# A fused attention, mixture-of-experts and gated-MLP kernel: another order of the first loads and of the first weight splits

## The chip, the cores and the metric

The kernel runs on one core of a Trainium2 chip. The time is the device time of one execution in microseconds; three executions were timed, and one more was recorded by the profiler. The engines are PE (TensorE, with PEld for its weight loads), DVE (VectorE), ACT (ScalarE), POOL (GpSimd) and SP (SyncE, which here only issues transfers).

## The reference

Causal attention with a bias from running sums of s, then four experts of which every token takes a share, then a gated MLP:

```python
scores = scale * np.matmul(q, k.transpose(0, 1, 3, 2))        # batch 2, 8 heads, 576 rows, 64 wide
cum = np.cumsum(np.maximum(s, 0.0), axis=-1)
bias = -(cum[:, :, :, None] - cum[:, :, None, :])
scores = np.where(causal, -1e9, scores + np.minimum(bias, 0.0))
attn = softmax(scores); x = (attn @ v) as [1152, 512]
for e in range(4):
    h = np.maximum(x @ w1[e], 0.0)                             # w1 512 x 1024
    out += p[:, e:e + 1] * (h @ w2[e])                         # p: domain_probs, each row divided by its sum
result = (out @ w_a) * (out @ w_b) @ w_out                     # 512 x 1536, 512 x 1536, 1536 x 512
```

## The kernel before

Nearly all products are made of three matmuls on float32r operands: each factor is split into a high part (ACT copies it to the narrow type) and a low part (DVE or POOL subtracts the high part from the original). For a weight piece of 512 KB, loaded into a tile `raw`, these are `wh` (ACT, line 225) and `wl` (line 227, two subtractions of 128x512, by turns on POOL and on DVE). The program runs in four parts.

**The head** (lines 722 to 908) computes the attention of the first 256 rows of batch 0 for all eight heads: `head_scores` (sc, lines 770 and 773), `head_softmax` (lines 784 and 788), `head_turn` (transposes into `tr`, line 796, and a copy, 799 or 801), `head_av` (809), and for every second head `pair_out` (821 to 834), which divides, transposes (`xT`, 829, in a PSUM tile of the pool of `tr`) and leaves the rows of x in plain form (`x32`) and split (`xh`, `xl`). Beside it `sums_of_s` (line 838 on) makes the running sums of s for the other rows: four short operations on DVE (845 to 857), four on POOL, and three writes to a scratch tensor `ckD` in DRAM (867). The head's own sums are made first (746 to 755, with the high and low part in `cb`). Small matmuls on a constant tile (`lull`, line 712) keep PE occupied in between.

**Beside** (from about 26 us): expert 0 on those 256 rows with plain fp32 weights (`plain_expert`, line 1010, weights `w32` loaded at line 556), then expert 1, and interleaved with both the attention of all other rows. That attention is 24 jobs (three groups of rows by eight heads), each of two or three query tiles. For a job `load_job` fetches `qr`, `kr` (one buffer each, lines 565 and 566) and the bias rows of `kb` (from `ckD`, 567); `prep_job` makes `qh`, `qb`, `ks` (572 to 579) and writes the high part of k into `kb` by a transfer from SBUF to SBUF (`kb<-ks`, line 578); `load_v` fetches `vr`. A tile's scores are two matmuls for each part: line 605 with `ks`, and line 606 with `kb`, which adds the low part and the bias. Then follow a softmax (DVE line 616, ACT 628, 633, DVE 634, POOL 635), transposes (646), their split (661, 662) and the product with v (678).

**After**: expert 1 on the last rows, then experts 0, 2 and 3, then the gated MLP.

The order on each engine is set by a list scheduler from the order in which the code records the operations and from their estimated times. `in_order` (and `queued`, while `early[0]` is set) keeps operations in the order in which they were recorded among themselves. `issue_after` holds what is recorded under it until a named operation has been issued; in the kernel before, a block at the end holds the weight loads of `w2`, the first three raw pieces and `prep_job` of the first job until the last `pair_out`, and `attn_step` does so for the first three steps of the attention. PE, DVE, ACT, POOL and the queue on SP each run their list strictly from front to back.

The block of code that the change turns round, as it stands before:

```python
    early[0] = True
    load_job(jobs[0])
    load_v(jobs[0])
    load_job(jobs[1])
    with tc.issue_after(last["act"].ins), tc.issue_after(last["dve"].ins):
        queued(nc.sync.dma_start(out=pr, in_=dp))
        for m in range(2):
            load_w32("w2", m)
        for _ in range(3):
            load_next()
        prep_job(jobs[0])
        early[0] = False
        shares()
```

## Time and profile before

| | before |
|---|---|
| median of 3 runs | 756.69 us (755.91 to 764.51) |
| the profiled execution | 756.76 us, of it 755.0 us from the first to the last instruction |
| busy: PE, DVE, ACT, POOL | 715.8, 515.2, 324.6, 401.4 us |
| mean granted clock of PE | 0.982 of full speed |

The profiled execution's time is the span between its first and last instruction and 1.76 us around it. It lies 0.07 us above the median. PE is busy for 95% of the span. In the page's strip of 40 slices its share is 9 tenths nearly everywhere but for three slices early on, of which the lowest holds 2 tenths; there the granted clock is 5 and 9 tenths. Busy shares are means over very different stages, so the tables below go by stage.

### The profile page before, as it was taken

To read this page: it belongs to the slowest core of one execution; us is meant where nothing else is said; L and a number is where in the kernel's file an instruction comes from. 1 tells how busy PE (TensorE), PEld (TensorE's weight loads), DVE (VectorE), ACT (ScalarE), POOL (GpSimd) and SP (SyncE) were. 2 spreads that over 40 slices of the span, in tenths; PEclk is the share of its full clock that TensorE was granted. 3 is DMA by queue.
4 is the path that set the end of the run, shared out by engine and by line. 5 is a ranking of instruction groups with operands and counts; after the bars stand their busy time and mean duration, and the time that the engine had idled before them with its cause. 6 is when DMAs were issued, how large, how long until landed. Compare 5 with 4: busy or idle time off the path is not lost.

```text
span 755.0 us, 10970 instructions
## 1 busy us (share of the span) xinstructions
PE 715.8 (95%) x3880; PEld 623.7 (83%) x3880; DVE 515.2 (68%) x1056; ACT 324.6 (43%) x722; POOL 401.4 (53%) x332
## 2 busy tenths in 40 slices
PE   9628899999999999999999999999899999999998
PEld 5527679899989988888888888887788888898886
DVE  5317678876768677766565646679874788887764
ACT  4327778987743433222321323243545324242410
POOL 4336665765524553333312345598467779798600
PEclk9959999999999999999999999999999999999999
DMA  6284423344221131111101112123103132223003
GB/s 225 70 283 135 122 76 102 98 139 112 66 67 44 50 101 52 62 56 56 48 9 56 57 56 84 56 85 94 47 28 95 61 97 73 93 63 104 5 0 126
DMA packets 33580, 61.42 MB, mean 81 GB/s; under 512 B 3269, under 2 KB 17253, under 8 KB 33525
## 3 DMA queue, kind: packets, MB, share of 16 engines
q1 hardware_dynamic: 33045, 59.61, 25.4%
q10 hardware_dynamic: 480, 1.11, 0.4%
q8 instruction: 31, 0.51, 0.3%
q14 instruction: 24, 0.20, 0.1%
HBM read 55.11 MB, written 2.58 MB: 76 GB/s over the span
## 4 chain that ended last, share of the span: by engine, by line
PE 61%; DVE 14%; POOL 8%; issue 5%; ACT 3%; DMA 1%; POOLq 0%; ACTq 0%; DVEq 0%; SPq 0%
PE ps L269 29%; PE psq L269 19%; PE pst L269 4%; POOL wl L81 3%; PE av L678 3%; PE tr L646 2%; PE ps L1010 1%; POOL tp L162 1%; DVE tp L174 1%; DVE tp L170 1%; DVE h2l L81 1%; PE sc L605 1%; PE sc L606 1%; DVE acc L1185 1%; DVE tp L166 1%
## 5 line engine op out<-in xcount | busy, mean ns | idle before, releaser
L269 PE MATMUL ps<-wh,h2h 128*128 128x512 f32 x332 | 130.6, 393 | 0.0
L269 PE MATMUL ps<-wl,h2h 128*128 128x512 f32 x332 | 129.6, 390 | 0.0
L81 POOL TENSOR_TENSOR wl<-raw,wh 128x1024 fp32r<-128x1024 f32 x24 | 58.1, 2431 | 129.3 <-ACT wh L80 98.9
L269 PE MATMUL ps<-wh,h2l 128*128 128x512 f32 x332 | 125.8, 392 | 0.8 <-DVE h2l L81 0.8
L322 DVE SCALAR_TENSOR_TENSOR acc<-ps,pr,acc 128x512 f32<-128x512 f32 x111 | 82.2, 745 | 41.4 <-PE ps L269 40.7
L269 PE MATMUL psq<-xh,wh 128*128 128x448 f32 (+1 forms) x224 | 81.5, 364 | 0.0
L269 PE MATMUL psq<-xl,wh 128*128 128x448 f32 (+1 forms) x224 | 81.3, 363 | 0.0
L269 PE MATMUL psq<-xh,wl 128*128 128x448 f32 (+1 forms) x224 | 81.2, 363 | 0.0
L269 PEld LDWEIGHTS ps<-wh,h2l 128*128 128x128 f32 x332 | 62.2, 188 | 14.7 <-DVE h2l L81 1.6
L269 PEld LDWEIGHTS ps<-wh,h2h 128*128 128x128 f32 x332 | 62.4, 188 | 11.8 <-ACT h2h L80 0.3
L269 PEld LDWEIGHTS ps<-wl,h2h 128*128 128x128 f32 x332 | 62.4, 188 | 11.1
L333 ACT ACTIVATE h2h<-psq 128x448 fp32r<-128x448 f32 (+1 forms) x56 | 29.5, 531 | 96.0 <-PE psq L269 77.2
L81 POOL TENSOR_TENSOR wl<-sums,wh 128x1024 fp32r<-128x1024 f32 x24 | 58.2, 2423 | 4.9 <-ACT wh L80 4.8
L635 POOL TENSOR_SCALAR e<-e,r 128x448 f32<-128x448 f32 (+4 forms) x64 | 37.6, 591 | 36.0 <-DVE r L634 25.9
L80 ACT ACTIVATE wh<-raw 128x1024 fp32r<-128x1024 f32 x24 | 25.5, 1062 | 70.3 <-PE ps L269 53.5
L269 PE MATMUL psq<-tqh,wh 128*128 128x448 f32 x144 | 53.0, 368 | 1.8 <-DVE u L420 1.2
L269 PE MATMUL psq<-tql,wh 128*128 128x448 f32 x144 | 52.6, 365 | 0.0
L269 PE MATMUL psq<-tqh,wl 128*128 128x448 f32 x144 | 52.5, 364 | 0.0
L662 DVE TENSOR_TENSOR el<-tr,eh 128x512 fp32r<-128x512 f32 (+5 forms) x80 | 38.5, 484 | 18.2 <-ACT eh L661 17.4
L162 POOL TENSOR_SCALAR tp<-tp 128x512 f32<-128x512 f32 x24 | 47.3, 1986 | 5.6 <-ACT tp L161 5.6
L269 PE MATMUL pst<-xh,wh 128*128 128x256 f32 x160 | 44.9, 280 | 2.7 <-DVE xl L81 2.7
L420 DVE TENSOR_TENSOR u<-psq,s 128x448 f32<-128x448 f32 x48 | 29.6, 618 | 23.9 <-PE psq L269 22.3
(198 smaller groups left out, 1898.4 us busy)
## 6 DMA issues: line engine op xcount, KB each, us to landing
raw<-in_w SPq DMA_DIRECT2D x32, 512.0 KB
raw<-in_wa SPq DMA_DIRECT2D x12, 512.0 KB
raw<-in_wb SPq DMA_DIRECT2D x12, 512.0 KB
raw<-in_wo SPq DMA_DIRECT2D x12, 512.0 KB
kr<-in_kT SPq DMA_DIRECT2D x16, 288.0 KB
w<-in_w SPq DMA_DIRECT2D x8, 512.0 KB
vr<-in_v SPq DMA_DIRECT2D x16, 160.0 KB
kb<-ks SPq DMA_DIRECT2D x16, 144.0 KB
```

The source lines that it names most:

```text
L80: nc.scalar.activation(out=hi, in_=src, func=AF.Copy)
L81: lo_eng.tensor_tensor(out=lo, in0=src, in1=hi.bitcast(F32), op=ALU.subtract)
L162: nc.gpsimd.tensor_scalar(out=t.bitcast(F32), in0=t.bitcast(F32), scalar1=2.0**-15, scalar2=GMAX, op0=ALU.max, op1=ALU.min,)
L166: nc.vector.tensor_scalar(out=t, in0=t, scalar1=5, scalar2=2, op0=ALU.logical_shift_left, op1=ALU.logical_shift_right,)
L269: ins = nc.tensor.matmul(ps, lhsT=l, rhs=r, start=first and k == 0, stop=last and k == 2, skip_group_check=more)
L322: nc.vector.scalar_tensor_tensor(out=dst, in0=ps, scalar=share, in1=dst, op0=ALU.mult, op1=ALU.add)
L333: nc.scalar.activation(out=hh, in_=src, func=AF.Relu)
L420: nc.vector.tensor_tensor(out=out, in0=a, in1=b, op=ALU.add)
L635: nc.gpsimd.tensor_scalar(out=t.e, in0=t.e, scalar1=r, scalar2=1.0, op0=ALU.mult, op1=ALU.mult)
L646: ins = nc.tensor.transpose(ps[:, c - c0, :], t.e[:, k0 : k0 + P], ident)
L662: nc.vector.tensor_tensor(out=j.el[:, c0:c1, x], in0=src, in1=hi.bitcast(F32), op=ALU.subtract)
L678: ins = nc.tensor.matmul(ps[:, o:], lhsT=j.vs[:, c, :], rhs=e[:, c, o:], start=(m == 0), stop=(m == len(mms) - 1),)
```

## The change

- **First loads.** The head's second load of s moves from the last to the first place on ACT's queue. All eight loads of `w32` (w1 and w2 of expert 0) are issued on SP at the start; before, the four of w2 came behind the head. The load of the shares (`pr`) and the first three raw pieces follow right behind the first job's loads, held no longer by the head's end. The second job's loads come after them, and after `prep_job` of the first job with its `kb<-ks`.
- **Held splits.** The splits of the first two raw pieces (`gated` in `split_next`) and the first three steps of the attention are held until the last `pair_out` has been issued. Transfers stay in the recorded order until the third step of the attention.
- **Sums of s.** `sums_of_s` is recorded after the first head's scores and before its softmax, before after the second head. One of the two short subtractions for `cb` goes from DVE to POOL.
- **Own bank.** `xT` takes a tile of the pool of `av` (one buffer), not of `tr`.

The diff, without repeated context:

```diff
+    gate = []
+    nsplits = [0]
+    def gated(on):
+        x = ExitStack()
+        for i in gate if on else ():
+            x.enter_context(tc.issue_after(i))
+        return x
...
     def split_next():
         r, p_ = loaded.pop(0)
-        split_piece(r, *p_)
+        nsplits[0] += 1
+        with gated(nsplits[0] < 3):
+            split_piece(r, *p_)
...
     in_order(nc.sync.dma_start(out=sc[:, :NT0], in_=s[:, :NT0]))
+    in_order(nc.scalar.dma_start(out=sc[:NR, NT0:], in_=s[:NR, NT0:]))
...
     in_order(nc.scalar.dma_start(out=v65, in_=v0))
-    in_order(nc.scalar.dma_start(out=sc[:NR, NT0:], in_=s[:NR, NT0:]))
-    for m in range(2):
-        load_w32("w1", m)
+    early[0] = True
+    for key in ("w1", "w2"):
+        for m in range(2):
+            load_w32(key, m)
+    early[0] = False
...
-    for lo_ in (slice(32, NB), slice(96, NS)):
-        nc.vector.tensor_tensor(
+    for lo_, eng in ((slice(32, NB), nc.vector), (slice(96, NS), nc.gpsimd)):
+        in_order(eng.tensor_tensor(
...
-        ps = ps_t.tile([P, NT0], F32, tag="tr", name="xT")
+        ps = ps_a.tile([P, NT0], F32, tag="av", name="xT")
...
         if h < H:
             head_scores(h)
+        if h == 0:
+            sums_of_s()
+        if h < H:
             head_softmax(h)
...
-        if h == 1:
-            sums_of_s()
...
-        if n > 2:
-            attn_work(n)
-            return
-        with tc.issue_after(last["act"].ins), tc.issue_after(last["dve"].ins):
+        early[0] = early[0] and n < 3
+        with gated(n < 3):
             attn_work(n)
...
     load_job(jobs[0])
     load_v(jobs[0])
-    load_job(jobs[1])
+    queued(nc.sync.dma_start(out=pr, in_=dp))
+    for _ in range(3):
+        load_next()
     with tc.issue_after(last["act"].ins), tc.issue_after(last["dve"].ins):
-        queued(nc.sync.dma_start(out=pr, in_=dp))
-        for m in range(2):
-            load_w32("w2", m)
-        for _ in range(3):
-            load_next()
         prep_job(jobs[0])
-        early[0] = False
+        load_job(jobs[1])
         shares()
+    gate.extend((last["act"].ins, last["dve"].ins))
```

Two places of the resulting order carry the prediction. The first is SP's queue behind the writes of `ckD`. The names are those of the text above with the batch, head and tile behind them: `kb_0_2` belongs to the first job, `kb_1_2` to the second. Before:

```order
L567 DMA kb_0_2_421<-ckD 3x576
L585 DMA vr_0_2_425<-in_v 128x320
L565 DMA qr_1_2_428<-in_qT 128x384
L566 DMA kr_1_2_429<-in_kT 128x576
L567 DMA kb_1_2_430<-ckD 3x576
L1198 DMA pr<-in_dp 128x36
L556 DMA w_118<-in_w 128x1024 x2
L556 DMA w_119<-in_w 128x1024 x2
L156 DMA raw<-in_w 128x1024 x3
L578 DMA kb_0_2_421<-ks_0_2_449 64x576
L578 DMA kb_1_2_430<-ks_1_2_468 64x576
L565 DMA qr_2_2_475<-in_qT 128x384
```

With the change, from the same load on:

```order
L578 DMA kb_0_2_425<-ckD 3x576
L596 DMA vr_0_2_429<-in_v 128x320
L1209 DMA pr<-in_dp 128x36
L156 DMA raw<-in_w 128x1024 x3
L589 DMA kb_0_2_425<-ks_0_2_442 64x576
L576 DMA qr_1_2_449<-in_qT 128x384
L577 DMA kr_1_2_450<-in_kT 128x576
L578 DMA kb_1_2_451<-ckD 3x576
L589 DMA kb_1_2_451<-ks_1_2_468 64x576
L576 DMA qr_2_2_475<-in_qT 128x384
L577 DMA kr_2_2_476<-in_kT 128x576
L578 DMA kb_2_2_477<-ckD 3x576
```

The four loads of w2 are gone from this stretch (they stand at the queue's start), and the first job's `kb<-ks` has moved ahead of the second job's three loads; the three raw pieces are still ahead of it.

The second place is DVE behind the head, where the softmax of the first job's tiles (`e_0_2_2`, `e_0_2_3`, `e_0_2_4`) and the split of the second raw piece (`wl<-raw`) meet. Before:

```order
L573 SCALAR_TENSOR_TENSOR qb_83<-qr_1_2_428,qh_1_2_427 64x384
L877 TENSOR_SCALAR den<-den 128x9
L878 RECIPROCAL den<-den 128x9
L227 TENSOR_TENSOR wl<-raw,wh 128x512 x2
L616 ISA e_0_2_2_503,mn<-sc_0_2_2_481,causal 128x320
L616 ISA mn 128x1
L616 ISA e_0_2_3_525,mn<-sc_0_2_3_500,causal 128x448
L616 ISA mn 128x1
L634 RECIPROCAL r<-l 128x1 x2
```

With the change:

```order
L584 SCALAR_TENSOR_TENSOR qb_84<-qr_0_2_423,qh_0_2_422 64x384
L1040 TENSOR_SCALAR h_510<-ps_497 128x256
L627 ISA e_0_2_2_503,mn<-sc_0_2_2_481,causal 128x320
L627 ISA mn 128x1
L227 TENSOR_TENSOR wl<-raw,wh 128x512 x2
L627 ISA e_0_2_3_525,mn<-sc_0_2_3_500,causal 128x448
L627 ISA mn 128x1
L584 SCALAR_TENSOR_TENSOR qb_83<-qr_1_2_449,qh_1_2_448 64x384
L645 RECIPROCAL r<-l 128x1
L627 ISA e_0_2_4_556,mn<-sc_0_2_4_515,causal 128x320
L627 ISA mn 128x1
```

The split stood ahead of the first softmax and now stands between the first and the second; the second job's `qb` has gone behind both.

## Rows read from the trace of the kernel before

**Rows 1.** PE's waits over the whole run (us in total, times, longest).
```profile
PE sc L606 <- DMA kr<-in_kT: 17.9, 1, 17.9
PE sc L605 <- DVE mn L616: 4.7, 3, 2.2
...
PE tr L796 <- DVE eT L799: 0.7, 1, 0.7
```

**Rows 2.** Windows by stage (stretch: its us, engines' busy us, clock, DMA).
```profile
31.00:52.00 21.00, 1.60 (x8) 0.86 (x6) 3.34 (x7) 4.85 (x8) 8.18 (x13) 0.58 0.84 254
52.00:92.00 40.00, 35.03 (x168) 28.81 (x169) 26.20 (x76) 27.30 (x78) 24.30 (x26) 0.88 0.47 139
92.00:232.00 140.00, 136.90 (x930) 123.00 (x929) 105.73 (x331) 105.61 (x334) 79.16 (x103) 1.00 0.33 94
```

**Rows 3.** Timeline from 31 to 41 us (start, us, engine, line, operation).
```profile
31.22 0.68 ACT L577 ACTIVATE ks<-kr 128x576 fp32r<-128x576 f32 x1
...
32.03 1.39 POOL L579 TENSOR_TENSOR ks<-kr,ks 64x576 fp32r<-64x576 f32 x1 [0.31 <-ACT ks L577]
...
32.16 0.33 SPq L565 DMA_DIRECT2D qr<-in_qT  x1
33.45 0.33 SPq L566 DMA_DIRECT2D kr<-in_kT  x1
...
34.56 1.85 SPq L556 DMA_DIRECT2D w<-in_w  x4
34.59 0.52 ACT L572 ACTIVATE qh<-qr 128x384 fp32r<-128x384 f32 x1 [2.06 <-DMA qr<-in_qT]
...
36.15 0.68 ACT L577 ACTIVATE ks<-kr 128x576 fp32r<-128x576 f32 x1 [1.03 <-DMA kr<-in_kT]
...
36.46 2.60 SPq L156 DMA_DIRECT2D raw<-in_w  x3
...
39.10 1.38 SPq L578 DMA_DIRECT2D kb<-ks  x2
```

**Rows 4.** Windows of the two stretches in which the transfers are dense.
```profile
35.00:51.00 16.00, 0.00 (x0) 0.00 (x0) 2.02 (x5) 2.91 (x4) 5.19 (x10) 0.50 0.96 293
1.00:14.00 13.00, 12.42 (x57) 6.84 (x57) 7.36 (x29) 4.86 (x10) 5.69 (x19) 1.00 0.83 300
```

**Rows 5.** Timeline from 47 to 66 us.
```profile
47.20 2.48 POOL L227 TENSOR_TENSOR wl<-raw,wh 128x512 fp32r<-128x512 f32 x2 [7.33 <-ACT wh L225]
...
49.92 1.29 DVE L227 TENSOR_TENSOR wl<-raw,wh 128x512 fp32r<-128x512 f32 x2 [10.83 <-ACT wh L225]
...
51.97 0.98 PE L606 MATMUL sc<-kb,qb 67*128 67x320 f32 x2 [17.87 <-DMA kr<-in_kT]
...
60.54 0.40 PE L605 MATMUL sc<-ks,qh 128*128 128x320 f32 x1
...
61.07 2.96 POOL L227 TENSOR_TENSOR wl<-raw,wh 128x512 fp32r<-128x512 f32 x2
...
61.54 3.04 DVE L227 TENSOR_TENSOR wl<-raw,wh 128x512 fp32r<-128x512 f32 x2
...
65.44 0.39 PE L605 MATMUL sc<-ks,qh 128*128 128x256 f32 x1 [1.50 <-DVE mn L616]
```

**Rows 6.** Windows of 4 us from 52 to 84 us.
```profile
52.00:56.00 4.00, 4.00 (x10) 3.33 (x11) 1.37 (x6) 2.12 (x8) 1.08 (x2) 0.50 0.64 215
56.00:60.00 4.00, 4.00 (x17) 3.46 (x17) 1.79 (x6) 2.00 (x4) 1.66 (x3) 0.71 0.16 45
...
80.00:84.00 4.00, 2.82 (x14) 2.64 (x15) 3.85 (x15) 2.06 (x6) 1.68 (x3) 0.77 0.43 140
```

**Rows 7.** Timeline of VectorE in the head, 8 to 12 us.
```profile
8.13 0.29 DVE L784 CUSTOM_DVE_ANT_0 e<-sc,causal 128x128 f32<-128x128 f32 x1 [1.91 <-PE sc L773]
...
9.96 0.32 DVE L845 TENSOR_SCALAR s_sb<-s_sb 32x320 f32<-32x320 f32 x1 [0.63 <-DMA s_sb<-in_s]
...
11.96 0.27 DVE L784 CUSTOM_DVE_ANT_0 e<-sc,causal 128x128 f32<-128x128 f32 x1
```

More of the change, by code (lines that the diff above doesn't have):

```diff
@@ L750, in fused_kernel @@
     )
-    nc.vector.tensor_scalar(
+    in_order(nc.vector.tensor_scalar(
         out=cb, in0=cum[:NS, :NT0], scalar1=1.0, scalar2=1.0, op0=ALU.mult, op1=ALU.mult
-    )
-    for lo_ in (slice(32, NB), slice(96, NS)):
-        nc.vector.tensor_tensor(
+    ))
+    for lo_, eng in ((slice(32, NB), nc.vector), (slice(96, NS), nc.gpsimd)):
+        in_order(eng.tensor_tensor(
             out=cb[lo_], in0=cum[lo_, :NT0], in1=cb[lo_].bitcast(F32), op=ALU.subtract
-        )
+        ))
     nc.gpsimd.memset(v65[:, :, :, D : D + 1], 1.0)
@@ L844, in sums_of_s @@
             )
-        nc.vector.tensor_scalar(
+        in_order(nc.vector.tensor_scalar(
             out=sc[:NR, NT0:], in0=sc[:NR, NT0:], scalar1=0.0, scalar2=None, op0=ALU.max
-        )
+        ))
         nc.vector.tensor_tensor_scan(
```

## The prediction

> **What bounds the kernel now.** I read PE's waits first, since PE is busy for 95% of the span: one wait stands out, 17.9 us before the first matmul of line 606, and the next longest is 4.7 us in three pieces [rows 1]. Then the windows by stage, to see where the hole lies. From 31 to 52 us PE works 1.60 of 21.00 us; from 52 to 92 us 35.03 of 40.00 us at a mean clock of 0.88; from 92 to 232 us 136.90 of 140.00 us at full clock [rows 2]. So the kernel is bound by PE, but for one hole and a ragged stretch behind it. What is taken out of the hole comes off the end as long as the other engines can follow.
>
> The trace names `kr<-in_kT` as what ended the wait. The matmul of line 606 reads no `kr`; it needs `kb`, `qb` and its bank. The timeline shows what it really waits for. `ks` of the first job is ready at 31.22 + 0.68 = 31.90 us, but SP issues `kb<-ks` only at 39.10 us, behind four loads of w2 (34.56) and three raw pieces (36.46), and PE goes on at 51.97 us [rows 3, 5]. From 35 to 51 us the DMA engines are busy for 0.96 of the time at 293 GB/s, that is 4.7 MB in 16 us [rows 4]; the seven weight transfers alone are 7 x 512 KB = 3.7 MB. A small transfer stands in line behind large ones, and PE behind it.
>
> **The change part by part.** All is counted against the profiled execution, 756.76 us (0.07 us above the median, so I use one figure for both).
>
> *The hole.* The order on SP puts `kb<-ks` of the first job ahead of the second job's loads, and w2 at the start. Is the line free when `ks` is ready? Up to 14 us the loads moved 13.0 us x 300 GB/s = 3.9 MB [rows 4]; 2.1 MB of w2 more at that rate take 7.0 us, until 21 us. The writes of `ckD`, the first job's loads and the three raw pieces, some 2.5 MB in all, take 8.4 us at 293 GB/s, until about 29.5 us even if nothing of them overlaps. So the line is empty at 31.9 us. The transfer itself (144 KB) has no undisturbed row. The nearest are a load of 192 KB, issued at 32.16 and used at 34.59 (2.43 us), and one of 288 KB, issued at 33.45 and used at 36.15 (2.70 us) [rows 3]. It is nearest in size to the first, but may run like the second, so line 606 starts at 34.3 to 34.6 us and not at 51.97. I take 17.5 us gained (17.3; at most the whole 17.9 of the wait).
>
> *The clock behind the hole.* With a hole of 2 us or less PE need not restart at half speed. From 52 to 56 us it ran 4.00 us at 0.50, from 56 to 60 us 4.00 us at 0.71 [rows 6]; at full clock the same work takes 2.0 and 2.84 us. That is 2.0 + 1.16 = 3.2 us gained, 0 if the new hole is long enough to drop the clock again.
>
> *Sums of s and the own bank.* In the head DVE sits idle for 1.91 us before the first softmax at 8.13 us. The sums start at 9.96 us, after 0.63 us of waiting for their load, and the next softmax follows at 11.96 us [rows 7]. Moved into the idle place, with their load issued first, they no longer hold up the heads behind: 11.96 - 9.96 = 2.0 us of work, which fits into 1.9 us of idle time, the more as one subtraction goes to POOL. The bank of `xT` may give another 0.7 us, the wait of a transpose for a bank [rows 1]. Other links of the head can take up part, so I take 1.8 us gained, nearest to the sums' row; 0 to 2.7.
>
> *The split that is now in line.* In the hole DVE made its first pair of `wl` at 49.92 us while PE stood still, and it cost nothing. Now the pair stands between the first and the second softmax of the first job, and the second softmax frees the bank that the third tile's scores need; all DVE work behind it waits too. Its price depends on POOL. POOL's first pair alone took 2.48 us and DVE's alone 1.29; when both ran at once DVE took 3.04 us and POOL 2.96 [rows 5]. With the change ACT releases the two pairs one after the other, POOL first, so they overlap in part. PE meanwhile has work of its own: five matmuls of line 1010 and the first half of the third tile. Ends: 0 if the pair takes 1.29 us, which that work covers, and 2.2 us if it holds PE as long as the longest wait of line 605 for a softmax [rows 1]; the next pair, at 61.54 us, held it for 1.50 us until 65.44 [rows 5]. I take 1.3 us lost, between the middle and that row.
>
> The trace shows both engines' pairs slowing each other. The Trainium skill ("GPSIMD Engine Reference", Specifications) says that GpSimd shares its SBUF interfaces with VectorE, with contention for VectorE instructions that have two SBUF inputs, and this subtraction is one: by that rule this term would lie at its upper end, by the undisturbed row at 0, and the trace bears the rule out (3.04 us against 1.29).
>
> *The second job's preparation and the rest of what lay in the hole.* The loads of the second job's `kr` still wait until POOL has read the first (issue at 33.45, landed at 36.15 us, the same as before [rows 3]). Its `ks` is then ready at 36.15 + 0.68 = 36.8 us, `kb` 2.43 us later at 39.3, and POOL's low part, 1.39 us long and behind POOL's pair of `wl`, by about 39 us [rows 3]. Before, PE came to the second job's scores 60.54 - 51.97 = 8.6 us after it had gone on [rows 5]; less 3.2 for the clock and with 1.3 for the split that is 6.7 us, at 41.0 us. So there are 2 us of cover. If that goes, what shows first is a wait of line 605 for POOL's `ks`. ACT, POOL and DVE have lost a place to work in. The hole held, from 35 us on, 2.91 us of ACT's, 5.19 of POOL's and 2.02 of DVE's work [rows 4], of which the shares on POOL have moved into the head. From 52 to 92 us they are busy for 61 to 68% [rows 2], so most of it finds room, but each piece that falls on the softmax chain shows. I take 1.5 us lost, between 0 and POOL's 5.2.
>
> *The rest* has one answer: the same weights, matmuls and splits are done in the same number; the `cb` subtraction on POOL ends before PE's constant matmuls do; and late in the program the scheduler deals some DVE and POOL steps in another order, worth 1.5 us either way.
>
> Sum: -17.5 - 3.2 - 1.8 + 1.3 + 1.5 = -19.7, so 756.8 - 19.7 = 737.1 us.
>
> **The rivals.**
>
> *The hole's work comes back.* If the softmax chain and not PE sets the pace behind the head, each split pair in line costs more than its own wait. The two pairs between 52 and 92 us account for 5.0 us of idle PE and about 1.6 us of lost clock beyond the restart (0.12 x 40 - 3.2), so 3.3 us a pair [rows 2, 6]. One pair more at that price, POOL's 5.2 us in full and no clock regained: -17.5 - 1.8 + 3.3 + 5.2 = -10.8, or 746.0 us. For it: DVE is at 3.85 of 4 us around 80 us [rows 6]. Against it: from 92 to 232 us the three engines carry shares of 57 to 76% and PE still works 98% [rows 2]. Chance 0.15.
>
> *The queue is still not empty.* Then `kb<-ks` waits for raw pieces that started late, since each load on SP waits for an earlier one to land. Each 512 KB ahead costs 0.52 MB / 293 GB/s = 1.8 us; all three leave 19.7 - 5.4 = 14.3 us, or 742.4 us. Against it speak the 2.4 us between 29.5 and 31.9, counted without overlap. Chance 0.06.
>
> *Slower: the clock stays low.* The gap behind the second pair's start follows a restart with little work on PE, and two more gaps follow; if the clock falls in the first and does not come back until PE is dense, the stretch that took 40 us (35.03 us of work at 0.88, 30.8 us at full clock) takes 61.6 us of PE time at 0.50. That is 21.6 us more against 19.3 gained, 759 us; it decides from 19.3 us of full-clock work run at half speed. Against it: after the gap of 1.50 us before 65.44 us [rows 5] the clock did not stay at half: 0.77 at 80 us is the lowest later stretch and 1.00 the mean from 92 us [rows 2, 6]. Chance 0.04. The rows show the clock at 0.50 through and behind the hole and back at 1.00 under dense work; the Trainium skill ("TensorE: Matmul & The Clock Gate", Part 1) has the throttled state as the default that activity releases, which is what this rival would need to go on for long, and the trace agrees with the rule but not with so long a stay.
>
> **How the numbers follow.** The forecast has 0.75. Its own range is 733 (2.7 from the head, nothing repaid, 1.5 us from the late order: 756.8 - 17.5 - 3.2 - 2.7 + 1.3 - 1.5 = 733.2) to 744 (no clock gain and 5.2 repaid: 756.8 - 17.5 - 1.8 + 1.3 + 5.2 = 744.0). The rival of the hole's work reaches 746.0, more often half of it, so 8 in 10 lie between 733 and 745 us. Two per cent, about what a measurement of this kernel can tell from no change, is 15.1 us: faster means below 741.6 us. The forecast lies below that except near its upper end (0.68 of its 0.75), with a small share of the two rivals on top (0.06); slower by over 2% (771.8 us) would need the low clock for 15 us more (0.01).
>
> **What would show it.** Right: SP issues `kb<-ks` within a microsecond of `ks`, PE's wait before the bias matmul of the first job is below 2 us, the matmul starts around 32.5 us, PEclk stays near full from 30 to 60 us; a first gap of 1 to 2 us appears behind DVE's pair of line 227; the softmax of the third head starts 2 us earlier; the stretch behind 230 us of before is the same, some 20 us earlier. The prediction would be wrong if line 606 or 605 still waited several microseconds for a transfer, if PE's idle time between 35 and 75 us added up to more than 8 us, or if the late part, where DVE and POOL steps stand in another order, lost more than 2 us.

## The result, and the profile after

The changed kernel takes 735.69 us (median of 4 runs, 734.1 to 736.0), the kernel before 756.72 (755.91 to 764.51). The ratio is 0.968, with an interval of 0.961 to 0.975; one run of before, at 764.51, lies apart and widens it, and one run each of e1 (746.31) and e3 (749.59), slow at a lower granted clock, is left out of their medians below. The forecast was 737.1 us with 733 to 745, so the time came out 1.4 us below it, inside the range. The profiled execution took 735.49 us, of it a span of 733.8.

PE's waits over the whole run (us in total, times, longest):

```profile
...
PE sc L617 <- DMA kr<-in_kT: 2.1, 1, 2.1
PE sc L616 <- POOL ks L590: 1.5, 1, 1.5
...
PE sc L616 <- DVE mn L627: 0.6, 1, 0.6
```

The wait of 17.9 us [rows 1] is gone (lines are 11 further down: 616 and 617 for the scores, 627 for the softmax). The wait of 2.1 us for a transfer is new; longer is only one of 2.7 us for `xl`, late in the program, as long as before. The first two windows of [rows 2] again:

```profile
31.00:52.00 21.00, 16.27 (x77) 13.77 (x78) 14.29 (x40) 14.97 (x38) 15.61 (x15) 0.90 0.72 208
52.00:92.00 40.00, 38.56 (x206) 29.27 (x205) 28.07 (x84) 31.90 (x88) 27.61 (x30) 0.96 0.39 108
```

From 31 to 52 us PE now works 16.27 us instead of 1.60. The timeline shows why:

```profile
30.25 0.68 ACT L588 ACTIVATE ks<-kr 128x576 fp32r<-128x576 f32 x1
30.96 0.56 SPq L589 DMA_DIRECT2D kb<-ks  x1
32.52 0.61 PE L616 MATMUL sc<-ks,qh 128*128 128x320 f32 x2 [1.53 <-POOL ks L590]
33.45 0.59 PE L617 MATMUL sc<-kb,qb 67*128 67x320 f32 x2 [0.32 <-issue]
34.29 2.59 DVE L227 TENSOR_TENSOR wl<-raw,wh 128x512 fp32r<-128x512 f32 x2
39.79 0.70 PE L616 MATMUL sc<-ks,qh 128*128 128x320 f32 x2
40.59 0.90 SPq L156 DMA_DIRECT2D raw<-in_w  x2
42.95 0.47 SPq L589 DMA_DIRECT2D kb<-ks  x1
50.12 0.58 PE L617 MATMUL sc<-kb,qb 67*128 67x320 f32 x2 [2.07 <-DMA kr<-in_kT]
```

`ks` is ready at 30.25 + 0.68 = 30.93, SP issues `kb<-ks` at 30.96, and the bias matmul runs at 33.45, where before the transfer was issued only at 39.10, 7.2 us after `ks` was ready, and PE stood until 51.97 [rows 3, 5]. The last three lines are the new wait: the third job's `kb<-ks` is issued at 42.95 behind two raw pieces (40.59), and PE goes on 7.2 us after that. (The trace names `kr` here too; in the second profile of this kernel, e14 below, it names `kb<-ks` for the same wait, 1.94 us.) PE's granted clock, in windows of 4 us as in [rows 6], still falls twice:

```profile
32.00:36.00 4.00, 3.17 (x11) 2.44 (x12) 2.13 (x4) 3.17 (x9) 3.92 (x4) 0.79 0.61 162
36.00:40.00 4.00, 4.00 (x18) 3.41 (x17) 3.85 (x11) 2.48 (x6) 2.64 (x4) 0.78 0.25 52
...
52.00:56.00 4.00, 4.00 (x18) 3.63 (x18) 1.13 (x5) 3.45 (x11) 2.66 (x4) 0.65 0.56 154
```

In the head the sums now sit where DVE was idle, as meant, but a longer wait has appeared further on. DVE, answering to [rows 7], and POOL:

```profile
5.15 0.32 DVE L859 TENSOR_SCALAR s_sb<-s_sb 32x320 f32<-32x320 f32 x1
8.00 0.29 DVE L798 CUSTOM_DVE_ANT_0 e<-sc,causal 128x128 f32<-128x128 f32 x1 [0.55 <-PE sc L787]
16.19 0.29 DVE L798 CUSTOM_DVE_ANT_0 e<-sc,causal 128x128 f32<-128x128 f32 x1 [3.53 <-PE av L823]
...
11.58 0.13 POOL L772 MEMSET va<- 128x16 f32 x1 [4.68 <-DMA va<-in_v]
14.77 1.39 POOL L879 TENSOR_TENSOR ckr<-dif,ckr 32x576 fp32r<-32x576 f32 x1
```

The fifth head's softmax (16.19) needs the buffer of `dif`, which POOL's chain for the sums frees at 14.77 + 1.39 = 16.16; that chain stands behind a memset that waits for the load of `va` until 11.58 (9.24 before). So the third head's softmax starts 2.1 us earlier than before (9.89 for 11.96), as forecast, and the fifth 2.3 us later (16.19 for 13.92).

### The profile page after: what moved, and what is told of

Read it like the earlier page. It is cut to its first block, busy times and chain, and to the rows that moved or that the text cites. A ratio compares the mean times of both kernels' runs of the same rounds, so it can differ in the third digit from the quotient of the medians.

```text
span 733.8 us, 10985 instructions
## 1 busy us (share of the span) xinstructions
PE 714.9 (97%) x3878; PEld 622.7 (85%) x3880; DVE 514.6 (70%) x1055; ACT 325.9 (44%) x722; POOL 402.6 (55%) x333
## 4 chain that ended last, share of the span: by engine, by line
PE 77%; DVE 7%; POOL 5%; ACT 4%; issue 3%; DMA 3%; POOLq 0%; SPq 0%; ACTq 0%; DVEq 0%
PE ps L280 32%; PE psq L280 26%; PE pst L280 6%; PE av L689 3%; PE tr L657 2%; PE ps L1023 2%; POOL wl L81 2%; DMA kr<-in_kT 2%; POOL tp L162 1%; PE sc L617 1%; PE lullps L723 1%; PE sc L616 1%; PE av L823 1%; DVE tp L170 1%; DVE tp L174 1%
```

## Where the 21 us come from

Two marks divide the run: the second job's first scores, and the first product of line 280 into `psq`, where expert 1's last rows begin and the attention's part is over (line 269 before). Both kernels do the same work up to each of the two; not up to the second job's scores, as said below the table.

| stretch | before | after | moved | forecast |
|---|---|---|---|---|
| start to the first scores | 33.48 | 32.52 | -0.96 | -1.8 |
| to the first bias matmul | 18.49 | 0.93 | -17.56 | -17.5 |
| to the second job's scores | 8.57 | 6.34 | -2.23 | -3.2 + 1.3 = -1.9 |
| to the first product into `psq` | 170.45 | 170.61 | +0.16 | +1.5 |
| to the end of the span | 524.0 | 523.4 | -0.6 | 0, 1.5 either way |

The sum is -21.2 us, against a forecast of -19.7. Of the third row's 2.23 us the order alone makes 0.69: before, seven transposes of the first job stand ahead of the second job's scores (60.54 [rows 5]), and in the changed kernel behind them.

```profile
59.85 0.93 PE L646 MATMUL tr<-ident,e 128*128 128x128 f32 x7
```

With the transposes counted in the fourth row for both, the third moved by -1.54 us (control, e14 below: -1.98) and the fourth by -0.53 (control -0.08).

## The experiments

Times of the marks in us, from the trace of each kernel; medians of 4 runs (of 3 in e1 and e3, of 10 in e8); before had medians of 756.72 to 757.89 beside them.

| run | first scores | first bias matmul | into `psq` | median (range) |
|---|---|---|---|---|
| before | 33.48 | 51.97 | 230.99 | 756.72 (755.91 to 764.51) |
| changed | 32.52 | 33.45 | 210.40 | 735.69 (734.1 to 736.0) |
| changed, again (e14) | 32.72 | 33.67 | 210.63 | 736.13 (734.12 to 737.48) |
| e1 memset of va last | 32.16 | 33.09 | 209.36 | 735.61 (734.67 to 735.88) |
| e2 raw behind third kb | 32.39 | 33.34 | 211.17 | 737.66 (734.8 to 739.12) |
| e3 e1 and e2 | 32.29 | 33.21 | 210.18 | 735.84 (735.73 to 738.7) |
| e4 before, first kb only | 32.85 | 36.72 | 215.89 | 744.19 (742.3 to 752.11) |
| e5 splits not held | 43.96 | 44.88 | 222.44 | 748.25 (746.73 to 748.95) |
| e6 fewer low parts | 32.20 | 33.16 | 209.81 | 737.0 (736.19 to 737.73) |
| e7 filled gap | 32.48 | 33.39 | 210.13 | 735.63 (734.99 to 738.17) |
| e8 head undone | 49.86 | 50.79 | 226.58 | 752.17 (750.3 to 757.64) |
| e9 w2 late | 29.92 | 30.92 | 212.37 | 737.81 (735.78 to 738.48) |
| e10 half raw loads | 32.65 | 33.62 | 213.92 | 737.51 (737.2 to 741.27) |
| e11 e8, s first | 34.54 | 35.47 | 210.07 | 738.34 (736.99 to 742.33) |
| e12 fourth raw buffer | 32.23 | 33.14 | 212.42 | 739.69 (739.15 to 740.16) |
| e13 w2 behind first job | 30.05 | 31.40 | 207.82 | 734.21 (733.49 to 735.02) |
| e15 first pairs on POOL | 32.21 | 33.17 | 218.78 | 745.38 (744.22 to 746.85) |

**The control.** e14 is the changed kernel, unaltered.

> The changed kernel once more, as a control: a second profile of the same instructions. If two profiles agree to 0.3 us at the first scores (32.52), at the first product into psq (210.40) and at the end of the span (733.8), differences of 0.5 us between kernels mean something; if the clock's dips and the waits on transfers move it by 1 us or more, they do not.

At the first scores and at `psq` the two profiles agree to 0.2 us. From `psq` to the end this one took 735.8 - 210.63 = 525.2 us against 523.4: the late part scatters by 1.8 us, so the 0.6 us in the table above are no gain, and the marks tell more than the medians. At `psq` I take differences above half a microsecond as real, with two reserves. A new order of the instructions behind an edit comes with each kernel. And each mark is read from one execution, which can be an untypical one: that of e10 took 741.27 us, its other three 737.2 to 737.56, so e10's marks tell little.

**Is it the line?** e4 is the kernel before, with the first job's preparation ahead of w2 and the raw pieces:

```diff
     with tc.issue_after(last["act"].ins), tc.issue_after(last["dve"].ins):
+        prep_job(jobs[0])
         queued(nc.sync.dma_start(out=pr, in_=dp))
...
-        prep_job(jobs[0])
         early[0] = False
```

> The kernel before with one edit: the preparation of the first job with its kb<-ks is recorded ahead of the loads of w2 and of the raw pieces, which stay behind the head; everything else as before. Theory A (a small transfer stands in line behind large ones): the first job's bias matmul starts at about 37 us and not at 51.97, but the second job's kb<-ks now stands behind the same 3.7 MB, so PE waits before the second job's line 606 until 48 to 51 us; the hole is moved by one job, and the time is 749 to 753 us. Rival (the first transfer alone was the matter, and its place in the queue is all that the change needed): the hole is gone and the time is 739 to 743 us.

From its timeline, the transfers on SP and the first bias matmul of each of the two jobs:

```profile
33.56 0.56 SPq L578 DMA_DIRECT2D kb<-ks  x1
34.78 2.24 SPq L556 DMA_DIRECT2D w<-in_w  x4
37.07 2.08 SPq L156 DMA_DIRECT2D raw<-in_w  x3
39.25 0.48 SPq L578 DMA_DIRECT2D kb<-ks  x1
...
36.72 0.98 PE L606 MATMUL sc<-kb,qb 67*128 67x320 f32 x2 [3.25 <-DMA kb<-ks]
49.40 0.95 PE L606 MATMUL sc<-kb,qb 67*128 67x320 f32 x2
```

The transfer that goes first is used 3.2 us after its issue. The second job's, behind seven pieces of 512 KB, is not used until 49.40, but PE has the first job's transposes and products in between and does not stand for it; the only other wait for such a transfer is 1.5 us, for a later job. So the line is what made the hole, and the hole did not move on to the second job, as I had it: `psq` comes 15.1 us earlier than before. Here my own theory fell and the rival held, nearly to its time. The changed kernel is another 5.5 us ahead at `psq`.

**Are the parts separable?** e5 takes away the hold on the first two splits:

```diff
-        with gated(nsplits[0] < 3):
+        with gated(False):
             split_piece(r, *p_)
```

> The changed kernel, but the splits of the first two raw pieces are not held until the last pair of heads. DVE's pair of line 227 then stands in the head, ahead of a copy of transposes and of the third pair of heads, and not between the first two softmaxes of the attention. Theory A (the pair in line behind the head costs what the prediction gave it, 1.3 us, and in the head it delays what stands behind it by its own 1.3 to 2.6 us): the first scores come at 33.5 to 35 us (32.52 in the changed kernel), the way from the bias matmul to the second job's scores is about 1 us shorter (6.34), and the time is 735.5 to 737 us. Rival (PE sets the pace of the head, as the run with the later memset has it, and the pair finds room there): the first scores stay at 32.2 to 32.8 us and the time is 733.5 to 735 us.

Both missed. First scores at 43.96, `psq` 12.0 us later. ACT and DVE in its timeline, and the first of PE's waits:

```profile
26.59 2.23 ACT L225 ACTIVATE wh<-raw 128x1024 fp32r<-128x1024 f32 x2 [5.70 <-DMA raw<-in_w]
28.86 2.36 DVE L227 TENSOR_TENSOR wl<-raw,wh 128x512 fp32r<-128x512 f32 x2 [6.23 <-ACT wh L225]
```

```profile
PE av L823 <- DVE eT L813: 8.1, 1, 8.1
```

The pair is not dear by its 2.36 us of work. It is dear because it stands in DVE's list ahead of a copy that the head needs, and its piece has not landed: ACT waits for the load, DVE for ACT, PE for DVE. So in this kernel the pieces can be loaded this early only with the hold.

e8 puts the code of the head back as it was, here its main lines (both `cb` subtractions are on DVE again as well); e11 is e8 with the load of s first, as changed:

```diff
-        if h == 0:
-            sums_of_s()
...
+        if h == 1:
+            sums_of_s()
...
-        ps = ps_a.tile([P, NT0], F32, tag="av", name="xT")
+        ps = ps_t.tile([P, NT0], F32, tag="tr", name="xT")
...
-    in_order(nc.scalar.dma_start(out=sc[:NR, NT0:], in_=s[:NR, NT0:]))
...
     in_order(nc.scalar.dma_start(out=v65, in_=v0))
+    in_order(nc.scalar.dma_start(out=sc[:NR, NT0:], in_=s[:NR, NT0:]))
```

```diff
     in_order(nc.sync.dma_start(out=sc[:, :NT0], in_=s[:, :NT0]))
+    in_order(nc.scalar.dma_start(out=sc[:NR, NT0:], in_=s[:NR, NT0:]))
...
     in_order(nc.scalar.dma_start(out=v65, in_=v0))
-    in_order(nc.scalar.dma_start(out=sc[:NR, NT0:], in_=s[:NR, NT0:]))
```

> The changed kernel with the head as before: the sums of s behind the second head, their load last on ACT's queue, both subtractions for cb on DVE, and xT in the pool of tr; the order of the weight loads and the held splits stay as changed. The prediction's term (1.8 us): the first scores come at 34.3 us, and the time is 737 to 738 us. Rival (only PE's own idle pieces of the head, 0.20 + 0.65 + 0.42 us before, can be won, since PE sets its pace): 33.3 to 33.8 us and 736 to 737 us.

> The run with the head as before, with one line as changed: the second load of s stands first on ACT's queue. Theory A (in that run the load came last on the queue behind the early loads of w2, landed at 9.19 us, held DVE's sums and with them the first softmax, PE stood for 3.09 us, and its clock fell to 0.50 and came back only at 44 us): the sums start before 7 us, PE's wait ahead of the third head's scores is below 1 us, the clock stays at 1.00, the first scores come at 32.5 to 34.0 us, and the time is 736 to 738.5 us. Rival (the early loads of w2 slow the whole head of before, or the place of the sums and the bank of xT matter by themselves): first scores beyond 36 us, and 740 us or more.

In e8 the first scores come 17.3 us late, beyond both of its expectations, in e11 2.0. DVE's wait for the load in e8's timeline and its first softmax, the first of PE's waits, and windows:

```profile
9.19 0.32 DVE L859 TENSOR_SCALAR s_sb<-s_sb 32x320 f32<-32x320 f32 x1 [2.40 <-DMA s_sb<-in_s]
...
10.71 0.29 DVE L798 CUSTOM_DVE_ANT_0 e<-sc,causal 128x128 f32<-128x128 f32 x1
```

```profile
PE sc L784 <- DVE mn L798: 3.1, 1, 3.1
```

```profile
8.00:12.00 4.00, 0.91 (x6) 0.61 (x7) 2.61 (x13) 0.96 (x3) 0.13 (x1) 1.00 1.03 410
12.00:16.00 4.00, 4.00 (x14) 2.33 (x14) 1.39 (x8) 1.95 (x6) 3.33 (x4) 0.53 1.03 410
...
36.00:40.00 4.00, 3.67 (x18) 3.36 (x19) 0.96 (x4) 1.15 (x3) 0.73 (x1) 0.50 0.00 0
...
44.00:48.00 4.00, 3.94 (x22) 3.15 (x21) 1.32 (x6) 1.37 (x4) 1.33 (x5) 1.00 0.00 0
```

The small load, last on its queue, holds DVE's sums, the sums hold the first softmax, PE stands for 3.1 us, and its clock falls to 0.50 and stays there until 40 us: the head then runs at half speed. With the load first e11 has a clock of 1.00 from 8 to 72 us. So theory A of e11 holds for the head (its first scores, at 34.54, lie half a microsecond beyond its range), and the price of "the head" is 17 us or 2 us, by one line. One part of the theory falls: the early loads of w2 did not delay this load. In the kernel before, without them, it let the sums go on at 9.96 us [rows 7], later than here. But there the first two heads' softmaxes stand ahead of the sums on DVE (8.13 us), and in e8, from the same code, the scheduler puts the sums first. So e8 has not the head of before; why the order differs was not tested. At `psq` even these 2 us are gone (210.07); the median, 2.6 us above that of the changed kernel, must then come from behind that mark or from executions that have no profile.

**Where w2 stands.** e9 and e13 move the four loads of w2 from the start, to behind the second job's loads (e9) or between the first job's loads and the raw pieces (e13, shown; in e9 the two lines stand behind `load_job(jobs[1])`):

```diff
-    for key in ("w1", "w2"):
-        for m in range(2):
-            load_w32(key, m)
+    for m in range(2):
+        load_w32("w1", m)
...
     queued(nc.sync.dma_start(out=pr, in_=dp))
+    for m in range(2):
+        load_w32("w2", m)
     for _ in range(3):
         load_next()
```

> The changed kernel, but the four loads of w2 (2 MB) are issued behind the second job's loads, not at the start; all else as changed. Theory A (the DMA engines are what is short from 40 to 52 us, where they are busy for 0.94 to 1.00 of the time; 2 MB more there take some 7 us, part of it beside PE's other work, as in the run with only the first kb<-ks moved): PE waits 1 to 5 us for the second or third job's kb<-ks, and the time is 737 to 742 us. Rival (w2 at the start was not needed, since the line is free for the first kb<-ks anyway): 734.5 to 736 us, with the first scores at the same 32.5 us.

> The changed kernel, but the four loads of w2 stand behind the first job's loads and ahead of the three raw pieces, so that they neither crowd the head's loads nor follow the first kb<-ks. Seven pieces of 512 KB from about 17 us take 12.2 us at 300 GB/s, until about 29.5 us. Theory A: the first scores come at 30 to 31 us, as in the run with w2 late (29.92), the first kb<-ks (issued at 28.4) lands by 32 us, and 1 to 2.5 us of this arrive at the end: 733 to 735 us. Rival (the stretch from 33 to 60 us takes up a gain of 2 us whatever it is, since there the transfers and the softmax chain have to catch up): the first scores come early, but the first product into psq stays at 209.5 to 211 us, and the time at 735 to 737 us.

Both heads are 2.5 to 2.6 us shorter. e9 gives it back, as its theory A had it, before the second job's bias matmul:

```profile
30.62 1.75 SPq L567 DMA_DIRECT2D w<-in_w  x4
36.09 0.48 SPq L589 DMA_DIRECT2D kb<-ks  x1
44.13 0.98 PE L617 MATMUL sc<-kb,qb 67*128 67x320 f32 x2 [4.95 <-DMA kb<-ks]
```

e13 keeps it, as its theory A had it, since the first `kb<-ks`, behind its seven pieces, is used 2.9 us after its issue:

```profile
18.10 2.60 SPq L567 DMA_DIRECT2D w<-in_w  x4
20.74 1.45 SPq L156 DMA_DIRECT2D raw<-in_w  x3
28.49 0.55 SPq L589 DMA_DIRECT2D kb<-ks  x1
...
31.40 0.59 PE L617 MATMUL sc<-kb,qb 67*128 67x320 f32 x2 [0.73 <-DMA kb<-ks]
```

At `psq` it is 2.6 us ahead of the changed kernel and 2.8 ahead of the control, as much as its head gained, and its median of 734.21 lies 1.9 us below the control's on the same chip. It is the one version here whose median is more than 1 us below the changed kernel's. But its range (733.49 to 735.02) overlaps that of the changed kernel's eight runs (734.1 to 737.48), and its ratio to before is the same 0.968 (0.961 to 0.976): the gain is likely, by the mark and the median, and not shown by the times. e1 tries the shorter way to the same gain, POOL's memset behind the sums:

```diff
-    nc.gpsimd.memset(v65[:, :, :, D : D + 1], 1.0)
...
         in_order(nc.gpsimd.tensor_tensor(out=lo, in0=dif, in1=mid.bitcast(F32), op=ALU.subtract))
+        in_order(nc.gpsimd.memset(v65[:, :, :, D : D + 1], 1.0))
```

> The changed kernel, but POOL writes the ones into the tile va (a short memset that needs the load of va) behind the four operations that make the running sums of s, and not ahead of them. Theory A: in the changed kernel the memset waits for the load of va until 11.58 us, the four operations therefore end at 16.16 us, and the softmax of the fifth head, which needs their buffer, stands until 16.19 us. Then it starts at about 13.1 us here, the first scores of the attention at 30.0 to 31.0 us (32.52 in the changed kernel), and the time is 733 to 734 us. Rival: the head's pace is set by its own chain of scores, softmax, transposes and products, and the early loads of w2 only crowd the DMA engines; then the fifth softmax starts earlier but the first scores stay at 32.0 to 32.6 us, and the time stays at 735 to 736 us.

The fifth softmax starts at 12.92 and not at 16.19, and the first scores come only 0.36 us earlier: its rival held, and PE's list, nearly the same as in the changed kernel, sets the pace of the head. (At `psq` e1 is 1.0 us ahead, but not in its median.) In e13 PE's list itself is another (two heads' scores stand together), and the load of `va` keeps the memset until 11.49 us there, as in the changed kernel (11.58). So that the early w2 crowds the head's loads is not shown; how much of the 2.5 us is the list and how much the loads was not taken apart.

**What sets the pace from 33 to 60 us.** Seven runs change something there. e2 holds the fourth and fifth raw pieces until the third job's `kb<-ks` has been issued; e3 is e1 and e2; e12 adds a fourth raw buffer to e2. e7 fills PE's gap before the first scores, e6 and e10 leave out parts of the work, e15 moves the first pairs to POOL. The edits of e2, e7, e6, e10 and e15, in this order (e12: the pool `raw` has 4 buffers and that of h 9, and four pieces are loaded at first):

```diff
-        if pieces and can_load():
-            load_next()
+        if pieces and can_load() and state["n"] > 3:
+            with tc.issue_after(last["kb"].ins) if nsplits[0] < 4 else ExitStack():
+                load_next()
...
-        queued(nc.sync.dma_start(out=j.kb[:D].bitcast(F32), in_=j.ks[:D].bitcast(F32)))
+        last["kb"] = queued(nc.sync.dma_start(out=j.kb[:D].bitcast(F32), in_=j.ks[:D].bitcast(F32)))
```

```diff
             t.ps.append((ps, c0, c1))
+            for _ in range(10 if len(passed) == 1 else 0):
+                nc.tensor.matmul(ps, lhsT=j.qh[:, q0 : q0 + P], rhs=j.qh[:, : c1 - c0], start=True, stop=True)
```

```diff
             slabs[key] = place_of(form)
+            if key in (("w1", 2), ("w1", 3)):
+                slabs[key] = (slabs[key][0],) * 2
...
-            for m in (2 * j, 2 * j + 1):
+            for m in (2 * j, 2 * j + 1) if wl is not wh else ():
```

```diff
+    nload = [0]
...
+        nload[0] += 1
+        if 3 < nload[0] < 9:
+            queued(nc.sync.dma_start(out=r[:, :1], in_=a[:, :1]))
+            return r[:, :1].broadcast_to(shape)
```

```diff
-            lo_eng = nc.gpsimd if nsplit[0] % 2 or nsplit[0] <= NFIRST else nc.vector
+            lo_eng = nc.gpsimd if nsplit[0] % 2 or nsplit[0] <= 4 else nc.vector
```

> The changed kernel, but the fourth and fifth raw pieces are issued behind the third job's kb<-ks, not ahead of it. Theory A: in the changed kernel this transfer stands in line behind them (issued at 42.95, landed at about 50.05 us), PE waits 2.07 us for it and the clock falls to 0.65 behind that. Then the wait before the third job's line 617 is below 0.5 us here, the clock does not fall at 52 to 56 us, and the time is 731.5 to 733.5 us. Rival: the transfer is slow because the DMA engines are full of other loads anyway, or the pieces are missed later by the splits; then a wait of about 2 us stays or appears elsewhere before 70 us, and the time is 735 to 737 us.

> Both edits, the memset of va behind the sums and the two raw pieces behind the third job's kb<-ks. If both theories hold and the gains add up: 729 to 731.5 us. If the head's gain is absorbed by a wait for the first job's preparation: 732 to 733 us. If both fall: 735 to 736 us.

> The changed kernel with ten more matmuls on qh of the first job, written to the bank of its first scores and overwritten by them; they fill PE's gap of 1.53 us ahead of the first scores. Theory A: the gap is what lets the clock fall to 0.79 from 32 to 40 us; without it the clock stays at 1.00 there, which gives back 0.21 x 3.2 + 0.22 x 4.0 = 1.5 us, and the time is 733.5 to 734.5 us. Theory B: the clock stays high but the softmax chain, not PE, sets the pace behind, as in the run with the later memset (clock 1.00 from 31 to 92 us and only some 0.7 us gained beyond the head): 735 to 736 us.

> The changed kernel without the low part of expert 1's two w1 slabs: the eight subtractions of line 227 for the first four raw pieces are left out (two pairs on POOL, two on DVE), and the matmuls read the high part in their place, so PE's work stays the same. It prices what the splits cost from 33 to 70 us. Theory A (PE sets the pace behind the head and the splits find room, as the small repayment in the changed kernel suggests): 734.5 to 736 us, and at the end of the attention's part (first product of line 280 into psq, at 210.40 us in the changed kernel) less than 1 us gained. Theory B (the chain of softmax and splits over DVE, ACT and POOL sets the pace there, which is why the removal of the third job's wait gave nothing): 3 to 6 us gained at that place, 730 to 733 us.

> The changed kernel, but the fourth to the eighth raw pieces load only their first half (256 KB) and the split reads that half twice, so that engine work and instructions stay the same and 1.3 MB of transfers between 40 and 70 us are left out. Theory C (the transfers, not PE, the clock or the splits, set the pace from 40 to 60 us): the third job's kb<-ks lands 2 us or more earlier, PE's wait of 2.07 us before line 617 is gone, and the end of the attention's part (first product into psq, 210.40 us in the changed kernel) comes 2 to 4 us earlier; 732 to 734 us. Rival (the chain of softmax work over DVE, ACT and POOL sets the pace; then this gives as little as the filled gap and the missing low parts did, 0.3 and 0.6 us at that place): 735 to 736 us.

> An attempt to beat both kernels: the changed kernel with a fourth raw buffer (the pool of h has 9 in place of 11 buffers), a fourth raw piece loaded while the DMA engines are idle (28 to 32 us), and the next raw pieces held behind the third job's kb<-ks. Theory C (transfers set the pace from 40 to 60 us): 731 to 734 us. Rival (softmax chain, or the two missing buffers of h, or the same megabytes a little later): 735 to 738 us.

> The changed kernel with the low parts of the first four raw pieces all on POOL, none on DVE, so that no pair of line 227 stands between the first softmaxes on DVE. Theory A (a pair in line on DVE holds the softmax that frees PE's bank; the prediction gave it 1.3 us a pair): no wait of line 616 for DVE's mn before 60 us, and the first product into psq 0.5 to 2 us earlier than 210.40. Rival (POOL, which has 4 x 2.5 us of pairs and the low parts of ks in one line, becomes the engine that is late): waits for POOL's ks or e appear, and the time is 736 to 739 us.

PE's clock is the clearest. The control and e7 have 1.00 from 32 to 48 us, the changed kernel 0.79 and 0.78 from 32 to 40, and all three are at the same place at `psq` (210.63, 210.13, 210.40). The control shows where it goes, in its windows and in its timeline:

```profile
32.00:36.00 4.00, 2.95 (x13) 2.42 (x14) 1.90 (x4) 3.24 (x9) 3.92 (x4) 1.00 0.61 162
36.00:40.00 4.00, 3.04 (x16) 2.33 (x15) 3.85 (x11) 2.53 (x6) 2.81 (x3) 1.00 0.24 44
```

```profile
34.51 2.57 DVE L227 TENSOR_TENSOR wl<-raw,wh 128x512 fp32r<-128x512 f32 x2
37.01 0.61 DVE L627 CUSTOM_DVE_ANT_0 e<-sc,causal 128x448 f32<-128x448 f32 x1
37.55 1.22 DVE L584 SCALAR_TENSOR_TENSOR qb<-qr,qh 64x384 fp32r<-64x384 f32 x1
37.69 0.39 PE L616 MATMUL sc<-ks,qh 128*128 128x256 f32 x1 [0.96 <-DVE mn L627]
39.57 0.84 PE L616 MATMUL sc<-ks,qh 128*128 128x320 f32 x2
```

DVE is busy for 3.85 of 4 us from 36 to 40. At full clock PE comes to the next scores earlier and waits 0.96 us for the softmax that stands behind the pair; the second job's scores then start at 39.57, against 39.79 with the clock down. So DVE's list, more than PE, sets the pace there; e7's theory B held.

The other runs give no gain either. e2 removes the third job's wait (its bias matmul at 46.59, not 50.12) and is 0.8 us later at `psq`; e3 is level; e6, with the first four low parts gone, gains 0.6, as its theory A had it; e12 loses 2.0, and e10, with 1.3 MB less to load, 3.5, of which much may be its untypical execution (clock 0.75, 0.50 and 0.90 from 60 to 72 us). e10 and e12 show the wait that the prediction feared, 3.2 and 4.8 us for DVE's `mn`; the changed kernel has 0.6 and the control 1.9, without a loss at `psq`. The medians of e2, e6, e10, e12 and e15 lie above all of their expected ranges.

e15 was to tell what happens without pairs on DVE. It does not, since its longest wait, 5.4 us where 8.4 were lost at `psq`, has another cause. The same stands in e6 (third line; line 227 there), where PE then waits 2.5 us:

```profile
50.16 1.06 ACT L225 ACTIVATE wh<-raw 128x1024 fp32r<-128x1024 f32 x1 [4.75 <-DMA raw<-in_w]
52.66 0.63 PE L689 MATMUL av<-eh,vs 128*128 128x320 f32 x1 [5.43 <-ACT eh L672]
```

```profile
47.46 1.06 ACT L227 ACTIVATE wh<-raw 128x1024 fp32r<-128x1024 f32 x1 [3.90 <-DMA raw<-in_w]
```

ACT stands for a raw piece that has not landed, with the softmax work behind it in its list, as in e5. So where splits come sooner, the transfers end last: in e15 the DMA engines are busy for 0.93 of the time at 290 GB/s from 48 to 52 us, while PE does nothing.

So no single theory of this stretch stands. PE's clock from 32 to 40 us is out. With the third job's transfer or with bytes out of the way, DVE's steps end last; with the low parts out of the way or off DVE, a raw piece does. That the place of a pair among the softmaxes decides more than its length is how I read this; each edit makes the scheduler place the pairs anew, so it is not shown. That e2 repays its 3.5 us is shown, and its cause is open (from 60 to 64 us it has PE at 2.47 of 4 us and a clock of 0.68).

## Where the prediction was right, and the step that failed

- **The hole** was read rightly, cause and size: -17.5 us forecast, -17.56 measured. The line was empty (no transfers from 28 to 32 us), and the transfer was used 2.5 us after its issue (30.96 to 33.45), within the estimate of 2.4 to 2.7. e4 shows that the place in the line alone brings 15 us.
- **The step that failed** is the last term of the sum, the rest of what lay in the hole: 1.5 us lost by forecast, 0.16 us measured, and with the seven transposes counted alike 0.53 us gained (control 0.08 gained). I had ACT, POOL and DVE losing a place to work in, and PE paying for part of it. The runs show otherwise. The fourth row's stretch in windows, before, changed and control (behind the limits stand its length and PE's busy time):

```profile
60.53:230.98 170.45, 162.38 (x1062) 143.49 (x1061) 127.76 (x394) 127.69 (x399) 99.16 (x125) 0.99 0.36 103
39.78:210.39 170.61, 163.28 (x1068) 144.13 (x1067) 124.01 (x396) 130.57 (x403) 100.72 (x127) 0.99 0.40 114
39.56:210.62 171.06, 161.97 (x1068) 142.61 (x1067) 126.14 (x399) 130.57 (x403) 101.57 (x127) 1.00 0.40 114
```

PE is idle there for 8.07, 7.33 and 9.09 us: nothing beyond the scatter of two executions came back. The feared wait for POOL's `ks` is 0.83 us in the control and absent in the changed kernel. What did appear is a wait that the sum has not, 2.07 us for the third job's transfer, in a stretch that takes up that much either way (e2).

- **Luck in the sum.** That term is 2.0 us off by this count. The head, 0.84 us short of its forecast, and the clock and the pair, 0.36 short, take back more than half of it, and the late part gave 0.6: that the total is 1.4 us off is in part luck.
- **Clock and pair**, -1.9 forecast, came out right only in their sum, -1.54 us (control -1.98) without the transposes. The 3.2 us of the clock and the 1.3 of the pair are not two costs: in the control, with the clock up, PE waits 0.96 us for the softmax behind the pair; in the changed kernel's profile, with the clock at 0.79 and 0.78, it does not. That the clock would stay near full from 30 to 60 us failed in that profile (0.65 once more from 52 us) and held in the control.
- **The pair beside POOL.** It took 2.59 us, 1.29 alone [rows 5]. POOL's pair beside it took 2.96 us. The Trainium skill ("GPSIMD Engine Reference", Specifications) names this contention, and the trace agrees again; in waits of PE this pair cost nothing in the changed kernel's profile and 0.96 us in the control.
- **Sums and own bank**, -1.8 forecast, -0.96 measured. The third head's softmax did start 2.1 us earlier; that POOL's part of the sums would hold the fifth by 2.3 us was counted at nothing. But e1, without that wait, gains only 0.36 us at the first scores, so what took up the rest is open. With w2 elsewhere the head is 2.5 us shorter (e9, e13), by the loads or by the other order on PE.
- **What the prediction did not see**: the change's parts guard each other. I priced the head's part at 1.8 us and the hold on the splits as a small loss. In the changed order the head's part without its first line costs 17 us (e8) and the missing hold 12 us (e5). A sum over parts, each against the kernel before, has no place for this.
- **The rivals.** The hole's work came back by 0.2 us at most, not by 8.5; the queue was empty; the low clock lasted 8 us and, further on, 4 more. But the mechanism of the slower rival is real: e8 shows a clock that stays low for 24 us, at another place.
- **The late part** moved by -0.6 us (control +1.2), inside the 1.5 either way.

## What to carry to other kernels

When a reordering has several parts, ask of each what the others make it cover: a step whose input comes late holds everything behind it on its engine (the splits in e5, the sums in e8), so the place of a load, the place of its step and the hold on that step belong together. Undo one part at a time from the changed side, and read the order on each engine again, since the scheduler deals it anew: undoing the head's code did not bring back the head's order. Compare at a point in the program beyond which nothing differs, and see whether the profiled execution is a typical one; the late part alone scattered by 1.8 us here. A PE stall of 3.1 us cost some 15 us where the clock fell ahead of a stretch of small matmuls (e8 against e11), and a lower clock from 32 to 40 us cost nothing clear of scatter where DVE's list ended last.

## What the runs showed of the hardware

- In e8 the clock stood at 0.50 from 16 to 40 us while PE was busy for 3.67 to 4.00 of every 4 us with small matmuls (0.53 in the window before, 0.63 in the one behind); the head of e11, without the stall, kept 1.00. The Trainium skill ("TensorE: Matmul & The Clock Gate", Part 1) has activity release the throttle; in the rows the clock is back at 1.00 only from 44 us on.
- The same instructions ran at 0.79 and 0.78 in one execution and at 1.00 in another, from 32 to 40 us; at `psq` the two are 0.2 us apart.
- One transfer of 144 KB was used 2.5 us after its issue on an empty queue (30.96 to 33.45; in e9, where PE waited for it by the trace, 28.36 to 30.92), and 7.2 us behind two pieces of 512 KB and smaller loads (42.95 to 50.12).
- A subtraction of 64x384 (`qb`) took 0.55 us on DVE in the kernel before while POOL stood idle (35.15), and 1.21 and 1.22 us in the changed kernel and the control beside a low part of `ks` on POOL (37.34, 37.55). Beside a pair of `wl` on POOL it took 0.55 us in the one (41.64) and 1.69 in the other (41.89), so what stands beside it does not settle its time alone.
